# Attention followed by a soft mixture of experts on one core: weight loads spread evenly and cut into short packets, the first three pairs' steps as a written list, idle products on a tile of ones

## The chip, the cores and the metric

The kernel runs on one core of a Trainium2 chip. The metric is the device time of one execution in microseconds, lower is better; the median of the runs counts. TensorE (PE) multiplies, VectorE (DVE), ScalarE (ACT) and GpSimd (POOL) work on its results, and SyncE (SP) and POOL start transfers between the chip's main memory (DRAM) and the core's working memory.

## What is computed

```python
# q, k, v: (8 batches, 12 heads, 448 tokens, 64)
scores = scale * np.matmul(q, k.transpose(0, 1, 3, 2))
m = np.max(scores, axis=-1, keepdims=True)
e = np.exp(scores - m)
attn = e / (np.sum(e, axis=-1, keepdims=True) + np.exp(-m) + 1e-09)
x = np.matmul(attn, v)                       # regrouped to (3584, 768)

logits = x @ phi                             # 32 slots = 8 experts x 4
d = softmax of logits over the 3584 tokens;  c = softmax over the 32 slots
slot_input = d.T @ x                         # (8, 4, 768)
h = np.maximum(slot_input[e] @ w1[e], 0.0)   # w1: (8, 768, 1024)
slot_out[e] = h @ w2[e]                      # w2: (8, 1024, 768)
out = c @ slot_out                           # (3584, 768), float32
```

## The kernel before

**Pairs.** The 96 heads are handled as 48 pairs (`NPAIR`). A pair `n` passes through these steps, each a function that emits instructions at the place where it is called; the order on each engine is the order of the calls.

- `T(n)`, L240: 28 transposes on PE bring q and k into `ps_t`; ACT (L262) or DVE copies them out. Three pairs share one load of q, k and v (a group).
- `A(n, i)`, L273: score products (L284, L293, L303) of one block of 128 queries into `ps_a`, and a maximum over the keys on DVE (L286, L297, L306). Three `ps_a` buffers exist, so PE waits for DVE. `As(c)` takes the next `c` of these steps off the list `runs`.
- `W1(g)`, L309, on POOL, turns the maxima of a group of pairs into a bias; `W2(g)`, L331, transposes it on PE (`ps_m`); `W3(g)` copies it on ACT (`mT`) and forms `exp(-m)`.
- `Bk(n, i)`, L351: score products with keys on the partitions, plus a product that adds the bias (L366 and L369, or L395 and L398), in `ps_b`; ACT takes the exponential (L371, L401). Four buffers, shared with `T`, `W2` and `PX`. In the middle of the kernel an `A` step of a later pair is woven in (`mix`).
- `AV(n, i, qs)`, L420: products with v into the one `ps_av` buffer (L435), for each of four key blocks `i` six products for three blocks of queries and two for the last.
- `N1(n)`, L442: `ps_av` is copied to `ubuf` (L448). `N2(n)`: reciprocal on DVE, multiplications on POOL (L468, L478, L479). `PX(n)`: transposes of the result (L500) and an ACT copy (L506).
- `V(g)` copies a group's v on POOL.

`P(b)` is the part of the mixture that belongs to one batch (six pairs): logits (`ps_l`, L534), running maxima, exponentials, `slot_input` sums.

**Order.** Before the loop: 22 products on a zeroed tile `wm[0]` (L692), then `T(0)`, four `A`, `T(1)`, `W1(0)`, v, `T(2)`, `W2(0)`, `W3(0)`, and loads. Then a loop over slots `s` = 0 to 48 with two halves each; slot `s` does the `Bk` of pair `s`, the second half of `AV` and the `N1`, `N2` of pair `s - 1`, `A` of pairs some three ahead and, from slot 2 on, `T(s + 6)`. Slots 0 to 2 go through the same loop with special cases (`early`, `hs == 1`, `hs < 5`).

**Loads.** All loads that convert from float32 to bfloat16 are issued by POOL and run through one queue of the DMA engines (`gdma`); SP starts those that need no conversion. The 16 expert matrices are halves of six or eight rows per partition; eleven of them (`halves` 0 to 10: all w1 and w2 of experts 0 to 2) have their own place from the start, and are loaded in two parts each: number 0 before the loop, number `half_at[s]` in slots `s + 1`. The last five lie over the attention's buffers, as 40 rows per partition: they are loaded when these come free (`load_rows`, `rows_at`), and some are converted ahead into a DRAM tile (`stage_rows`, L141, its transfer L145, at the slots in `stage_at`) and later fetched from there by SP (`fetch_rows`, L153). w2 is read as `(p j) f`: a partition's rows follow each other in DRAM.

**The end.** After the attention come two groups of four experts: `hidden` (L848), `turn` (transposes of `h`, L860), `slots` (`ps_so`, L867), and the output rows (L904, L906, L910) with 13 stores by SP.

Of the kernel before, what the change touches and what calls it, by code (L numbers as in the profile page):

```python
# [8 lines left out]
F32 = mybir.dt.float32  # L9
# [22 lines left out]
def kernel(  # L32
# [77 lines left out]
    def load_part(i, z0, z1):  # L110
        kind, e = halves[i]
        src = (moe_w1 if kind == "w1" else moe_w2)[e].rearrange("(j p) f -> p j f" if kind == "w1" else "(p j) f -> p j f", p=128)
        gdma(out=w_sb[(kind, e)][:, z0:z1, :], in_=src[:, z0:z1, :])  # L113
# [27 lines left out]
    def stage_rows(r0, r1):  # L141
        i, z = divmod(r0, FK)
        assert r1 <= (i + 1) * FK
        t = dram.tile([128, r1 - r0, DD], BF16, name=f"stage{r0}")
        gdma(out=t, in_=moe_w2[11 + i - E].rearrange("(p j) f -> p j f", p=128)[:, z:z + r1 - r0, :])  # L145
        staged[r0, r1] = t
# [9 lines left out]
    with ExitStack() as at:  # L156
# [532 lines left out]

        ps = psV.tile([128, 512], F32, tag="v", name="ps_idle")  # L690
        for _ in range(22):
            nc.tensor.matmul(ps[:, 0:64], wm[0][:, 0, :], wm[0][:, 0, 0:64], start=True, stop=True)  # L692
        T(0)
        As(2)
        T(1)
        As(2)
        W1(0)
        V(0)
        load(1, "v")
        ones_in(vp[1], nc.gpsimd)  # L700
        As(1)
        T(2)
        W2(0)
        W3(0)
        As(1)
        for nm in "qk":
            load(2, nm)
        for z in range(2):
            load_half(0, z, w_tile(0))

        half_at = {s: i + 1 for i, s in enumerate((1, 4, 7, 10, 13, 19, 22, 28, 31, 34))}


        rows_at = {77: 3, 83: 7, 85: 12, 89: 17, 91: 20, 92: 24, 93: 26, 95: 27}
        rows = 0
        stage_at = {18: (16, 24), 37: (27, 32), 38: (32, 36), 40: (36, 40)}
        wait_loads = []
        waits = [r for z in stage_at.values() for r in range(*z)]  # L720
        for s in range(NPAIR + 1):
            for y in range(2):
                hs = 2 * s + y
                early = int(hs < 4)
                mix = s >= 3 and len(runs) > 1 and runs[0][1] == 1 - y
                if mix:
# [4 lines left out]
                if mix:  # L731
                    pass
                elif s < NPAIR:
                    Bk(s, 2 * y)
                    As(early)
                    side = int(y == 1 and len(runs) > 0 and runs[0][1] == 3)
                    Bk(s, 2 * y + 1, side)
                    As(1 - side)
                else:
                    As(1)  # L740
                if hs == 1:
                    W1(1)
                if hs < 5:
                    T(hs + 3)
                if y == 0:
                    if 0 <= s - 1:
                        for i in (2, 3):
                            AV(s - 1, i, range(3))
                else:
                    if 2 <= s < NPAIR - 6:  # L750
                        T(s + 6)
# [19 lines left out]
                else:  # L771
                    if 0 <= s - 1 and on_pool(s - 1):
                        N2(s - 1)
                As(early)
                if hs == 1:
                    W2(1)
                    W3(1)
                if y == 0 and s and s + 1 in firsts:
# [4 lines left out]
                if y == 0 and s % 3 == 2 and (s + 1) // 3 < NG:  # L783
                    if s == 2:
                        load(2, "v")
                    if s == NPAIR - 4:
                        V(NG - 1)
                    if s - 1 in half_at:
                        load_half(half_at[s - 1], 0, w_tile(half_at[s - 1]))
                if y == 0 and hs in rows_at:  # L790
                    load_rows(rows, rows_at[hs])
                    rows = rows_at[hs]
            def slot_loads(s):
                g = (s + 10) // 3
                if s == 1 or (s and s % 3 == 2):
                    if g < NG:
                        load(g, "q")
                        load(g, "k")
                g = (s + 9) // 3
                if s % 3 == 0 and g - 2 < NG - 1:  # L800
                    V(g - 2)
                    if s and g - 1 < NG:
                        load(g - 1, "v")
                if s - 1 in half_at:
                    load_half(half_at[s - 1], 1)
                if s in stage_at:
                    stage_rows(*stage_at[s])

            if s > 2 and s + 2 in firsts:
# [45 lines left out]
        def turn(g):  # L855
            n = FK // (1 + g)
            for k0 in range(0, FK, n):
                ps = psA.tile([128, n, 128], BF16, tag="a", name="ps_ht")
                for kt in range(k0, k0 + n):
                    nc.tensor.transpose(ps[:, kt - k0, :], h[g].rearrange("p (d k) -> p k d", k=FK)[:, kt, :], ident)  # L860
                (nc.scalar.copy if g and not k0 else nc.vector.tensor_copy)(hT[g][:, k0:k0 + n, :], ps)
# [155 lines left out]
```

## Time and profile before

| | |
|---|---|
| runs | 299.71, 300.39, 301.83 us; median 300.39 |
| profiled execution | 300.82 us, of which span (first to last instruction) 299.0 |
| busy of the span | PE 272.7, DVE 249.7, ACT 250.7, POOL 193.3 |
| maximum on DVE, one alone; six in a row | 0.615; 3.28 |
| 28 transposes, at 9.98 us; at 18.25 us | 0.96; 0.63 |
| exponential on ACT, L371; L401 | 0.575; 0.572 |
| software queue (q0) | 42.29 MB, 35072 packets |
| instruction queue (q8) | 0.66 MB, 40 packets |
| staging of rows 16 to 23 (L145) | 1536 KB, 13.0 us from issue to landing |
| expert weights, 24 transfers | 768 KB each, median 10.1 us to landing |

A timeline row gives the start (us from the span's start), the duration from the first to the last of its instructions, engine, line, operation, what is written and read, the count, and in brackets the engine's idle time before it and what ended that. "issue" stands where the profile names nothing that the engine waited for. A piece of the chain of waits has its start, its length, engine and line. PEld is the loading of PE's stationary operand.

### The profile page before, as it was taken

What the parts mean: (1) busy time and instruction counts of PE and PEld (TensorE: products, weight loads), DVE (VectorE), ACT (ScalarE), POOL (GpSimd) and SP (SyncE); (2) the same over time, 40 slices, a digit from 0 to 9 for tenths busy, and PEclk for the clock granted to TensorE, in tenths of its full rate; (3) what the DMA queues carried; (4) which work ended last, traced back from release to release, by engine and by line L of the source; (5) the groups of instructions that cost most, each with busy time, mean ns of one, the idle gap of its engine ahead of it and who ended that gap; (6) DMA issues with size and microseconds to landing.
All of it is one profiled execution on the core that took longest, in us unless ns stands there. A gap on an engine that the chain in (4) does not pass through costs nothing.

```text
span 299.0 us, 12393 instructions
## 1 busy us (share of the span) xinstructions
PE 272.7 (91%) x5174; PEld 162.8 (54%) x5174; DVE 249.7 (83%) x581; ACT 250.7 (84%) x559; POOL 193.3 (65%) x389
## 2 busy tenths in 40 slices
PE   5989999999999999899999999999999999996810
PEld 4434556565666566557566666666565556652100
DVE  5889799999999999899999999998999675437930
ACT  4567999999899989898999899989999987337820
POOL 8791997879778959886969697978775633000000
PEclk9999999999999999999999999999999999997555
DMA  7999799999999978999998999999999689808997
GB/s 137 142 145 208 115 207 207 209 207 207 193 189 171 197 101 120 193 189 207 210 153 113 151 192 162 194 178 207 181 196 197 120 177 266 329 4 323 380 448 322
DMA packets 40103, 58.67 MB, mean 196 GB/s; under 512 B 2752, under 2 KB 30912, under 8 KB 39744
## 3 DMA queue, kind: packets, MB, share of 16 engines
q0 software_dynamic: 35072, 42.29, 85.8%
q1 hardware_dynamic: 4976, 15.60, 13.3%
q8 instruction: 40, 0.66, 0.8%
q14 instruction: 15, 0.12, 0.1%
HBM read 89.16 MB, written 15.14 MB: 349 GB/s over the span
## 4 chain that ended last, share of the span: by engine, by line
PE 73%; ACT 11%; DVE 5%; issue 3%; POOL 2%; DMA 1%; DVEq 0%; POOLq 0%; ACTq 0%
PE ps_av L435 16%; PE ps_a L284 11%; PE ps_b L366 8%; PE ps_b L369 7%; PE ps_t L255 6%; PE ps_b L395 5%; PE ps_b L398 3%; PE ps_x L500 3%; PE ps_o L910 3%; ACT W L401 2%; ACT W L262 2%; DVE mx L297 2%; ACT W L506 2%; PE ps_s L622 2%; PE ps_h L848 2%
## 5 line engine op out<-in xcount | busy, mean ns | idle before, releaser
L286 DVE TENSOR_REDUCE mx<-ps_a 128x1 f32<-128x448 f32 x250 | 137.4, 613 | 5.2 <-PE ps_a L284 4.4
L371 ACT ACTIVATE W<-ps_b 128x448 bf16<-128x448 f32 x250 | 120.4, 575 | 0.0
L284 PE MATMUL ps_a<-W 64*128 64x448 bf16 x250 | 80.8, 352 | 0.1
L366 PE MATMUL ps_b<-W 64*128 64x448 bf16 x250 | 70.2, 352 | 1.3
L369 PE MATMUL ps_b<-mT,sel 64*128 64x448 bf16 x250 | 66.3, 350 | 0.1
L435 PEld LDWEIGHTS <-W 128*128 128x128 bf16 (+1 forms) x1536 | 50.3, 100 | 27.4 <-issue 23.6
L435 PE MATMUL ps_av<-W 128*128 128x65 bf16 (+1 forms) x1536 | 64.5, 196 | 0.3 <-issue 0.3
L468 POOL TENSOR_TENSOR W<-ubuf,rec 128x384 bf16<-128x384 f32 x44 | 36.3, 826 | 38.6 <-ACT W L506 19.2
L401 ACT ACTIVATE W<-ps_b 128x448 bf16<-128x448 f32 x86 | 45.5, 572 | 4.2 <-PE ps_b L398 4.2
L255 PEld LDWEIGHTS <-W 64*64 64x64 bf16 x1344 | 29.2, 112 | 13.0 <-issue 4.7
L506 ACT CAST W<-ps_x 128x512 bf16<-128x512 f32 x47 | 28.6, 607 | 6.4 <-PE ps_x L500 6.1
L255 PE MATMUL ps_t<-ident,W 64*64 64x64 bf16 x1330 | 30.4, 195 | 2.6 <-ACT W L214 1.3
L306 DVE TENSOR_REDUCE mx<-ps_a 128x1 f32<-128x448 f32 x48 | 29.5, 615 | 1.5 <-PE ps_a L303 1.5
L284 PEld LDWEIGHTS <-W 64*128 64x128 bf16 x250 | 23.3, 94 | 9.8
L369 PEld LDWEIGHTS <-sel 64*128 64x128 bf16 x250 | 19.5, 94 | 14.8 <-issue 6.0
L395 PE MATMUL ps_b<-W 64*64 64x448 bf16 (+1 forms) x134 | 26.9, 374 | 0.3
L113 POOL DMA_DIRECT2D W<-in_moe_w_dram x30 | 20.9, 698 | 7.7 <-PE ps_b L398 7.7
L262 ACT COPY W<-ps_t 128x896 bf16<-128x896 bf16 x21 | 19.6, 933 | 7.2 <-PE ps_t L255 7.2
L448 ACT COPY ubuf<-ps_av 128x455 f32<-128x455 f32 x44 | 25.1, 571 | 0.3
L398 PE MATMUL ps_b<-mT,sel 64*64 64x448 bf16 (+1 forms) x134 | 24.9, 354 | 0.2
L297 DVE TENSOR_REDUCE mx<-ps_a 128x1 f32<-128x448 f32 x38 | 20.9, 616 | 2.1 <-PE ps_a L293 2.1
L479 POOL TENSOR_TENSOR W<-ubuf,rec 128x128 bf16<-128x128 f32 x44 | 17.6, 400 | 3.7
(156 smaller groups left out, 447.2 us busy)
## 6 DMA issues: line engine op xcount, KB each, us to landing
W<-in_moe_w_dram POOLq DMA_DIRECT2D x24, 768.0 KB, 10.1
W<-in_v_dram POOLq DMA_DIRECT2D x32, 192.0 KB, 6.4
out_dram<-W SPq DMA_DIRECT2D x2, 2688.0 KB, 10.0
W<-in_q_dram POOLq DMA_DIRECT2D x15, 336.0 KB, 6.2
W<-in_k_dram POOLq DMA_DIRECT2D x15, 336.0 KB, 7.2
out_dram<-W SPq DMA_DIRECT2D x6, 384.0 KB, 3.0
out_dram<-W SPq DMA_DIRECT2D x3, 768.0 KB, 4.9
W<-stage SPq DMA_DIRECT2D x3, 576.0 KB, 5.6
```

The source lines that it names most:

```text
L255: nc.tensor.transpose(o, src[r, pl, tok * D:(tok + 1) * D], ident[r, r])
L284: nc.tensor.matmul(ps[:, 0:S], t[r, 0, i * 128:(i + 1) * 128], t[r, 1, :], start=True, stop=True)
L286: nc.vector.reduce_max(m[:, c:c + 1], ps[:, 0:S], axis=AX.X)
L366: nc.tensor.matmul(pss[hl][:, 0:S], t[rs[hl], 1, cols], t[rs[hl], 0, :], start=True, stop=False)
L369: nc.tensor.matmul(pss[hl][:, 0:S], sel[rs[hl], 2 * pl + hl:2 * pl + hl + 1].to_broadcast([64, 128]), mT[mg(n)][rs[hl], :], start=False, s ...
L371: nc.scalar.activation(e[:, hl, :], pss[hl][:, 0:S], AF.Exp, scale=scale)
L395: nc.tensor.matmul(outs[hl], t[rs[hl], 1, cols], t[rs[hl], 0, :], start=True, stop=False)
L398: nc.tensor.matmul(outs[hl], sel[rs[hl], 2 * pl + hl:2 * pl + hl + 1].to_broadcast([64, m]), mT[mg(n)][rs[hl], :], start=False, stop=True)
L401: nc.scalar.activation(e, p[:, 0:S], AF.Exp, scale=scale)
L435: nc.tensor.matmul(o, eT[n, i, hl][:, qc], vp[g % 2][:, 2 * pl + hl, i, 0:W65], start=(i == 0 and u == 0 and hl == 0) or (u == 3 and i == ...
L468: eng.tensor_mul(x[:, 0:3, c:c + 128].rearrange("p i (h d) -> p i h d", h=2), u[:, 0:6, 0:D].rearrange("p (i h) d -> p i h d", h=2), rec[: ...
L506: nc.scalar.copy(xT(b, pb), pss[0])
```

## The change

1. `load_part` reads w2 of experts 0 to 3 (halves 8 to 10, and rows 0 to 7 of the 40) as `(j p) f`: partition `p` has rows `p`, `128 + p`, and so on, so each packet is one row. `turn(0)` reads `h[0]` in the order that fits, contiguous columns instead of every eighth.
2. The DRAM tile of `stage_rows` gets 32 unused columns a row, so each of its rows is a packet of its own.
3. `half_at` is every third slot from 4 to 31 instead of ten slots from 1 to 34, and the second part of a half moves from the end of slot `s + 1` to the first half of slot `s + 2`. `stage_at` has the rows 16 to 23 at 34 instead of 18, in two pieces; rows 27 to 31 in two pieces; rows 32 to 39 at 40 in two pieces. First pieces go out in slot `s + 1`, second pieces in slot `s + 2`.
4. The 22 products on `wm[0]` become 48 on the program's constant tile of ones (written at the program's begin), and two of 128 columns follow `T(0)`.
5. The steps before the loop and slots 0 to 2 become one written list, `ramp`; the loop begins with slot 3.

```diff
-        src = (moe_w1 if kind == "w1" else moe_w2)[e].rearrange("(j p) f -> p j f" if kind == "w1" else "(p j) f -> p j f", p=128)
+        src = (moe_w1 if kind == "w1" else moe_w2)[e].rearrange(
+            "(j p) f -> p j f" if kind == "w1" or e < E // 2 else "(p j) f -> p j f", p=128)
...
-        t = dram.tile([128, r1 - r0, DD], BF16, name=f"stage{r0}")
+        t = dram.tile([128, r1 - r0, DD + 32], BF16, name=f"stage{r0}")[:, :, 0:DD]
...
-        ps = psV.tile([128, 512], F32, tag="v", name="ps_idle")
-        for _ in range(22):
-            nc.tensor.matmul(ps[:, 0:64], wm[0][:, 0, :], wm[0][:, 0, 0:64], start=True, stop=True)
-        T(0)
-        As(2)
-        T(1)
-        As(2)
-        W1(0)
-        V(0)
...
+        one = nc.const_aps.tensor(1.0, [128, 512], BF16)
+        ps_idle = psV.tile([128, 512], F32, tag="v", name="ps_idle")
+
+        def idle(n, cols):
+            for _ in range(n):
+                nc.tensor.matmul(ps_idle[:, 0:cols], one[:, 0:128], one[:, 0:cols], start=True, stop=True)
+
+        idle(48, 64)
...
-        half_at = {s: i + 1 for i, s in enumerate((1, 4, 7, 10, 13, 19, 22, 28, 31, 34))}
+        half_at = {s: i + 1 for i, s in enumerate(range(4, 32, 3))}
...
-        stage_at = {18: (16, 24), 37: (27, 32), 38: (32, 36), 40: (36, 40)}
+        stage_at = {34: [(16, 20), (20, 24)], 37: [(27, 29), (29, 32)], 40: [(32, 36), (36, 40)]}
...
+        ramp = ("T0 I A A T1 A A W0 T2 A G0 A X0 J0 A B0.0 A B0.1 A A T3 A B0.2 A A T4 C0.3 V0.0 W1 A V0.1 V0.2 A X1 T5 "
+                "A B1.0 A K0 V0.3 H0 C1.1 N0 B1.2 A T6 C1.3 V1.0 V1.1 A B2.0 M0 K1 A T7 B2.1 A V1.2 V1.3 W2 T8 H1 A "
+                "N1 B2.2 Y2 V2.0 X2 C2.3 Z0 V2.1 M1 K2 ")
...
-        for s in range(NPAIR + 1):
+        for s in range(3, NPAIR + 1):
...
+                if y == 0 and s - 1 in stage_at:
+                    stage_rows(*stage_at[s - 1][0])
+                if y == 0 and s - 2 in half_at:
+                    load_half(half_at[s - 2], 1)
+                if y == 0 and s - 2 in stage_at:
+                    stage_rows(*stage_at[s - 2][1])
...
-                if s - 1 in half_at:
-                    load_half(half_at[s - 1], 1)
-                if s in stage_at:
-                    stage_rows(*stage_at[s])
...
-                    nc.tensor.transpose(ps[:, kt - k0, :], h[g].rearrange("p (d k) -> p k d", k=FK)[:, kt, :], ident)
+                    nc.tensor.transpose(ps[:, kt - k0, :], h[g].rearrange("p (d k) -> p k d" if g else "p (k d) -> p k d", k=FK)[:, kt, :],
+                                    ident)
```

In the list `T`, `A`, `N` (`N1`), `M` (`N2`), `W` (`W1`) are the steps above, `X` is `W2` and `W3`, `B` a `Bk` and `C` a `Bk` with an `A` step inside, `V` an `AV` of three query blocks, `H` the four `AV` of the last query block, `I` the two idle products, `G` the copy of v for group 0 with the next load of v, `J` the loads of q and k of group 2 and of half 0, `K` a slot's loads, `Y` the load of v of group 2, `Z` the first `PX`.

## The prediction

> **What bounds the kernel now.** First the slices of the page: in each row a digit is the busy share of 1/40 of the span (7.5 us).
>
> ```profile
> PE   5989999999999999899999999999999999996810
> DVE  5889799999999999899999999998999675437930
> ACT  4567999999899989898999899989999987337820
> ```
>
> Three stretches: a start of four slices in which nobody is full, a long middle in which PE is full but for one slice (the 17th, near 125 us), and an end that the change hardly touches. Next the chain of waits, where the six logit products of each batch (`ps_l`, L534) come once every six pairs and so serve as a clock of the middle:
>
> ```profile
> 59.71 0.59 PE ps_l L534 x24
> ...
> 88.63 0.59 PE ps_l L534 x24
> ...
> 117.59 0.59 PE ps_l L534 x24
> ...
> 147.79 0.59 PE ps_l L534 x24
> ...
> 176.81 0.59 PE ps_l L534 x24
> ```
>
> The steps are 28.92, 28.96, 30.20 and 29.02 us: a steady PE pace of 4.83 us a pair, and one batch that lost 30.20 - 28.95 = 1.25 us. The timeline of that batch has the loss:
>
> ```profile
> 125.69 0.35 PE L255 MATMUL ps_t<-ident,W 64*64 64x64 bf16 x11 [0.87 <-issue]
> ...
> 127.06 3.28 DVE L286 TENSOR_REDUCE mx<-ps_a 128x1 f32<-128x448 f32 x6 [1.09 <-PE ps_a L284]
> ```
>
> PE stopped for 0.87 us in the middle of 28 transposes of data that had landed by 102. "issue" says that no engine and no load held it. In the packet records the instruction queue (q8, 16 KB a packet) asks every 6 to 7 us, but here it goes from 113.7 to 123.5; between lies the staging load of L145 (issued at 116.7, 1536 KB, 13.0 us to landing), whose packets are 32 KB, the largest of the run. I read it as PE waiting for its next instructions behind those packets.
>
> Last, VectorE in the start:
>
> ```profile
> 11.97 0.62 DVE L306 TENSOR_REDUCE mx<-ps_a 128x1 f32<-128x448 f32 x1 [0.92 <-PE ps_a L303]
> ...
> 20.98 3.28 DVE L297 TENSOR_REDUCE mx<-ps_a 128x1 f32<-128x448 f32 x6 [0.67 <-PE ps_a L293]
> 24.70 0.62 DVE L306 TENSOR_REDUCE mx<-ps_a 128x1 f32<-128x448 f32 x1 [0.43 <-PE ps_a L303]
> ...
> 31.92 1.16 DVE L297 TENSOR_REDUCE mx<-ps_a 128x1 f32<-128x448 f32 x2 [0.48 <-PE ps_a L293]
> ...
> 34.51 0.62 DVE L286 TENSOR_REDUCE mx<-ps_a 128x1 f32<-128x448 f32 x1 [0.60 <-PE ps_b L366]
> 35.63 1.16 DVE L286 TENSOR_REDUCE mx<-ps_a 128x1 f32<-128x448 f32 x2 [0.49 <-PE ps_a L284]
> ```
>
> From its first maximum (5.73) to 35.63 DVE does 46 maxima at a pitch of 0.547 us (six in 3.28) and two reciprocal steps, 25.7 us, and idles 4.2 us: the six gaps shown and 0.36, 0.18, 2 x 0.04. PE and ACT idle more (ACT 8.0 us from 8.20 to 29.36), then ACT has no gap at all from 29.36 past 36. So the start is DVE's queue, starved where PE has other work ahead of a score product, with ACT late at its end.
>
> **The list of first steps.** The work of pairs 0 to 2 is the same; from pair 3's first score product on, PE's order is that of before. So the start is worth what that point moves, and the PE-paced middle passes it on. Gap by gap: 0.36 is the landing of pair 1's k and stays. 0.92 came because 28 transposes (0.96) and the mask products stood between A(1,0) and A(1,3); now they stand behind A(0,1) and A(0,2), whose four maxima are 2.2 us of cover: gone. 0.18 and 0.67 came from W2(1), which waits for GpSimd's W1(1), itself behind four load issues until 19.69; the loads stay there, but A(3,1) and A(3,2) now stand ahead of W2(1): some 0.15 is left. 0.43 came from transposes and 20 value products ahead of A(4,3); these are now cut into sixes and twelves between A's: gone. The last three (1.57) come where ACT frees `ps_b` buffers late. ACT's work is no smaller: I worked the engines' queues through in program order with the rows' own pitches (maximum 0.547, exponential 0.425, transposed copy 0.80, pair of score products 0.19, 28 transposes 0.44, or 0.89 before 14 us, GpSimd's rows as they are, loads landing as they did). That puts the four copies of `ubuf` (L448; rows 24.47, 31.86, 37.18, 41.88) at 24.1, 31.3, 36.7, 41.4 for before, and at 23.8, 29.7, 34.5, 39.2 for the new order, with one DVE gap of 1.25 near 31, where A(6,3) waits behind pair 2's last scores for a buffer. Left are 0.36 + 0.15 + 1.25 = 1.75 of 4.2, a gain of 2.45; the copies give 2.2. I take **-2.3**. Bounds: -3.85 if only the 0.36 stays; 0 if ACT and the landings give all back, for T(6) and T(9) now come 0.5 and 0.4 us behind their landings (before: T(9) at 38.0).
>
> **Idle products.** 22 took 1.36 us, 0.055 each once running; 48 take 0.2 + 47 x 0.055 = 2.8 us. Their operand is written by GpSimd at 0.31 instead of DVE at 0.86, so they run from about 0.8 to 3.6, and T(0) waits for its cast until 3.82: hidden by 0.2 us; without that cover +0.2. The two of 128 columns (0.11 each) sit in PE's 0.39 us of waiting for the first copies. What they may bring is the clock. The page shows full clock from the start, but 28 transposes take 0.96 at 9.98 and 0.63 at 18.25, a lone score product 0.53 and then 0.35: the array is slow until about 14.5. By the same working, full speed from 7 instead of 14 moves the end of the start by 0.2, from 4 by 0.6, for DVE and the landing of q, k of group 1 (14.0) hold it anyway. I count 0.1 in the -2.3; bounds +0.2 and -0.6.
> [...]
>
> **Loads.** The staging of rows 16 to 23 moves from slot 18 to slots 35 and 36, in two halves; every staged row is now a 1536-byte packet; the w2 halves of experts 0 to 3 go from 6144 to 1536 bytes. The 32 KB packets are gone, so the 1.25 goes: **-1.2**. A smaller stop of 0.35 at 213.7 stands in the same kind of load (7680-byte packets): **-0.2**. Bounds: 0 (the stop has another cause) and -1.6. What replaces them: halves now go out every three slots from slot 4 to 31. The software queue runs one transfer after another: a half lands 3.7 us behind the one before it, q or k 1.7, v 1.0 twice; three slots need 2 x 3.7 + 2 x 1.7 + 2 x 1.0 = 12.8 of 14.5 us. Packet size hardly shows: 512 bytes at 195 GB/s, 896 at 200, 2048 and 6144 at 207 to 210. At 195 three slots need 13.3: hidden. If that cover went, the price would be what 14.5 is exceeded by, ten times; for 1 us a half must take 3.7 + 0.9. GpSimd issues 512 pieces for 128 (0.63 us; 384 pieces take 0.78, so some 0.85): six halves, expert 3's rows and the staging, +0.2 each on an engine 65% busy whose loads land far ahead: its next work behind them is N2, whose result PX needs a slot later. 0. The worst landing (k, 13.4 us, at 137.4) was still some 6 us ahead of its transposes. The rows (32, 36) and (36, 40) are staged 3 and 1 slots later; the queue stood empty near 238 to 240, which takes it. SP has one fetch more at 0.32.
> [...]
>
> **The end.** `h[0]` is transposed from contiguous columns instead of every eighth: eight take 0.71 in either group now, 0; bounds +-0.1.
>
> **Sum.** -2.3 - 1.2 - 0.2 = -3.7. The profiled execution took 300.82 (span 299.0, 1.8 around it), which gives 297.1; it lay 0.4 over the median 300.39, which gives **296.7**.
>
> **Rivals.**
> 1. The start gives it back: ACT, gapless from 29.36 on, or T(6) and T(9) at their landings, starve DVE as before. For it: the 1.25 gap that was worked out and the thin 0.4 to 0.5 us; against: the same working meets the rows of before within 0.5. Only the loads pay: -1.4, 299.0. Chance 0.13.
> 2. The stop stays or moves: the instruction queue still waits behind staging, now at slots 35 to 42. For: it has one packet every 6 to 7 us whatever the loads; against: the w2 halves with 6144 bytes show no stop. -2.4, 298.0. Chance 0.10.
> 3. More: DVE keeps only the 0.36 (-3.85), and the loads -1.4: 295.1. Against it is ACT's gapless stretch. Chance 0.12.
> 4. Slower: the last fetches. From 251 to 262 SP fetches 13 staged rows (2.6 MB) at some 400 GB/s, 6.4 us of transfer, and the second group's products use the last at about 266, 4 us after it landed. Rows now come as 1536-byte packets out of padded rows instead of 4.6 to 7.7 KB. At a third of the rate the 6.4 us become 19.2 and overrun by 8.8; with the -3.7 that is +5.1, 305.5. It costs below 250 GB/s and outweighs the gain below 180. Against: output stores are 1536-byte packets already, and 384 KB land 0.5 us after 192 KB do (3.0, 2.5), 390 GB/s. Chance 0.05.
>
> **Numbers.** The forecast has 0.60, reaching from 295.6 to 298.2 by the bounds of its terms. About 1% (3 us, 297.4) is what a measurement can tell; five sixths of the forecast lie under it, so faster 0.50 + 0.12 = 0.62; slower 0.05; the rest, 0.33, within. The range leaves out the slower case and some of the ends: 294.9 to 299.2.
>
> **What would show it.** Right: L448's first four copies near 23.9, 30.1, 35.0, 39.7; DVE idle under 2.3 us up to pair 3; the `ps_l` steps all within 28.8 to 29.1; no "issue" wait of PE over 0.3 in the middle. Wrong: a step still over 29.5; ACT or a landing releasing several DVE gaps before 30 us; `ps_so` products waiting for a load.

## The result, and the profile after

| | before | after |
|---|---|---|
| median (runs) | 300.45 us (20) | 298.94 us (20) |
| ratio, 95% interval | | 0.9946, 0.9924 to 0.9968 |
| profiled execution, span | 300.82, 299.0 | 300.67, 298.9 |

By the ratio, which compares the means of the runs without the few that lie over 1.5% above the fastest of their kernel, the change saves 1.6 us (1.0 to 2.3), where 3.7 were forecast. The profiled execution lies 1.7 us over the median of its kernel, so its lines show more waiting than most executions have; runs further below tell which of it belongs to the program.

The slices of the page, one digit for 7.5 us:

```profile
PE   7989899999999999999889999999999999996810
...
DVE  6999789999999989999889999999999675537930
ACT  4569989999899979998989899989999987337810
...
PEclk9599999999999999999999999999999999998555
```

PE's hole in the 17th slice is gone, and two new ones stand in the 20th and 21st (near 142 to 157 us). In the start the third slice has its 8 still, and the fifth (30 to 37 us) has an 8 where it was full. The clock row has full speed in the first slice and half of it in the second; the trace's record of the clock begins at 4.72 in this execution, and the row counts the time before it as full.

The chain of waits of the changed kernel (start, length, engine, line):

```profile
4.37 6.58 DMA W<-in_v_dram
...
17.55 7.30 DMA W<-in_k_dram
...
30.88 7.09 DMA W<-in_k_dram
...
59.15 0.59 PE ps_l L535 x24
...
88.07 0.59 PE ps_l L535 x24
...
117.68 0.59 PE ps_l L535 x24
...
147.15 0.59 PE ps_l L535 x24
...
177.50 0.59 PE ps_l L535 x24
```

Two things answer to the prediction. The chain now runs through the load of k of group 2 and that of group 3, transfers that the forecast had left as they were. And the first batch's logits come 0.56 us earlier (59.71 to 59.15), but the steps after that are 28.92, 29.61, 29.47 and 30.35, not 28.8 to 29.1: at 177.50 the kernel is 0.69 later than before.

The first four copies of `ubuf` by the timeline (forecast: 23.9, 30.1, 35.0, 39.7; before: 24.47, 31.86, 37.18, 41.88):

```profile
24.48 0.55 ACT L449 COPY ubuf<-ps_av 128x455 f32<-128x455 f32 x1
...
30.68 0.61 ACT L449 COPY ubuf<-ps_av 128x455 f32<-128x455 f32 x1
...
35.89 0.59 ACT L449 COPY ubuf<-ps_av 128x455 f32<-128x455 f32 x1
...
41.44 0.60 ACT L449 COPY ubuf<-ps_av 128x455 f32<-128x455 f32 x1
```

At the first copy nothing is won, at the second and third 1.2 to 1.3 us; at the fourth 0.44 are left. The gaps of VectorE there, in the same view:

```profile
10.00 1.16 DVE L298 TENSOR_REDUCE mx<-ps_a 128x1 f32<-128x448 f32 x2 [0.38 <-PE ps_a L294]
...
21.73 1.16 DVE L298 TENSOR_REDUCE mx<-ps_a 128x1 f32<-128x448 f32 x2 [0.31 <-PE ps_a L294]
...
30.45 1.16 DVE L298 TENSOR_REDUCE mx<-ps_a 128x1 f32<-128x448 f32 x2 [0.48 <-PE ps_a L294]
...
32.98 0.62 DVE L307 TENSOR_REDUCE mx<-ps_a 128x1 f32<-128x448 f32 x1 [1.37 <-PE ps_a L304]
```

Five of the six gaps that the prediction showed are gone or smaller. The sixth stands unchanged: 0.48 us ahead of the 43rd maximum, at 31.92 before and at 30.45 here. In all VectorE idles 2.9 us up to pair 3, where under 2.3 were forecast. A gap of 1.37 stands where the forecast expected one of 1.25, but its cause is another, as the first two rows of PE's own waits show:

```profile
31.34 0.34 PE L436 MATMUL ps_av<-W 128*128 128x65 bf16 x6 [0.62 <-ACT ubuf L449]
...
32.24 0.34 PE L336 MATMUL ps_m<-ident,W 128*128 128x128 bf16 x3 [0.56 <-POOL W L314]
...
38.01 0.41 PE L256 MATMUL ps_t<-ident,W 64*64 64x64 bf16 x14 [0.93 <-DMA W<-in_k_dram]
...
105.10 0.34 PE L336 MATMUL ps_m<-ident,W 128*128 128x128 bf16 x3 [0.58 <-POOL W L314]
...
142.72 0.35 PE L285 MATMUL ps_a<-W 64*128 64x448 bf16 x1 [0.44 <-DVE mx L287]
...
149.74 0.57 PE L256 MATMUL ps_t<-ident,W 64*64 64x64 bf16 x24 [0.52 <-issue]
...
156.21 0.22 PE L436 MATMUL ps_av<-W 128*128 128x65 bf16 x2 [0.58 <-issue]
```

These are a wait of `AV` for ACT's copy of `ps_av`, waits for GpSimd's bias (`W2`, twice), one for a landing (`T(9)`), and three stops in the middle, two of them with no releaser. None of the seven stands at its place in the profile of before. The first two lie ahead of the score product that ends the gap of 1.37 (L304, near 32.55). The prediction had that product wait behind pair 2's last scores for a buffer; here 0.56 of its delay is a wait for GpSimd that the forecast didn't have. That the size agrees is luck: without that wait the gap is 0.64 (e5_behind, below).

### The profile page after: what moved, and what is told of

Same layout as the page of the kernel before. It is cut to its first block, busy times and chain, and to the rows that moved or that the text cites. A ratio compares the mean times of both kernels' runs of the same rounds, so it can differ in the third digit from the quotient of the medians.

```text
span 298.9 us, 12454 instructions
## 1 busy us (share of the span) xinstructions
PE 271.9 (91%) x5202; PEld 164.0 (55%) x5202; DVE 249.5 (83%) x581; ACT 250.0 (84%) x559; POOL 196.1 (66%) x391
## 4 chain that ended last, share of the span: by engine, by line
PE 71%; ACT 9%; DMA 7%; POOL 5%; issue 3%; DVE 1%; DVEq 0%; POOLq 0%; ACTq 0%
PE ps_av L436 16%; PE ps_a L285 11%; PE ps_b L367 8%; PE ps_b L370 7%; PE ps_b L396 5%; DMA W<-in_k_dram 5%; PE ps_t L256 5%; PE ps_x L501 3%; PE ps_b L399 3%; PE ps_o L932 2%; DMA W<-in_v_dram 2%; ACT W L402 2%; PE ps_s L623 2%; PE ps_h L869 2%; ACT W L507 2%
## 5 line engine op out<-in xcount | busy, mean ns | idle before, releaser
L287 DVE TENSOR_REDUCE mx<-ps_a 128x1 f32<-128x448 f32 x250 | 137.2, 613 | 5.1 <-PE ps_a L285 4.3
L114 POOL DMA_DIRECT2D W<-in_moe_w_dram x30 | 22.6, 755 | 7.9 <-PE ps_b L399 7.7
L298 DVE TENSOR_REDUCE mx<-ps_a 128x1 f32<-128x448 f32 x38 | 21.2, 616 | 1.9 <-PE ps_a L294 1.8
```

The source lines that it names most:

```text
L287: nc.vector.reduce_max(m[:, c:c + 1], ps[:, 0:S], axis=AX.X)
```

## The experiments

Three theories stood after this. **A:** the list runs PE up against GpSimd's queue and the landings of groups 2 and 3, which caps the start. **B:** the stops in the middle are accidents of an execution that no load's shape removes, so the 1.4 us for the loads were never to be had. **C:** the clock, which rises early and falls back, takes the gain. The table has all runs; what they are follows below. "Eighth copy" is the start of the eighth copy of `ubuf` in that run's timeline, by which the start is over; "middle" is the time from the first batch's `ps_l` row to the seventh's; "stops" is the sum of PE's stops at a code boundary between 60 and 240 us (below).

| run | median | ratio to before, interval | eighth copy | middle | stops |
|---|---|---|---|---|---|
| before | 300.45 | | 60.64 | 174.6 | 1.22 |
| after | 298.94 | 0.9946 (0.9924 to 0.9968) | 60.08 | 175.2 | 1.54 |
| e8_again (after) | 298.67 | 0.9930 (0.9906 to 0.9954) | 60.03 | 174.0 | 0.60 |
| e1_loads | 300.25 | 0.9984 (0.9958 to 1.0011) | 60.55 | 173.4 | 0 |
| e2_list | 298.64 | 0.9930 (0.9898 to 0.9963) | 59.05 | 174.0 | 0.27 |
| e3_idle22 | 298.72 | 0.9947 (0.9915 to 0.9978) | 58.88 | 174.4 | 0.82 |
| e4_early | 298.17 | 0.9898 (0.9853 to 0.9943) | 58.14 | 174.8 | 1.33 |
| e13_before_early | 300.33 | 0.9961 (0.9930 to 0.9991) | 60.45 | 173.1 | 0 |
| e5_behind | 296.91 | 0.9880 (0.9853 to 0.9907) | 58.15 | 173.2 | 0.28 |
| e14_best (e5_behind) | 296.92 | 0.9858 (0.9822 to 0.9895) | 58.38 | 173.3 | 0.31 |
| e12_oldloads | 297.55 | 0.9880 (0.9840 to 0.9919) | 58.38 | 174.3 | 1.15 |
| e10_longpk | 297.62 | 0.9879 (0.9836 to 0.9922) | 59.88 | 173.9 | 0.76 |
| e9_idle57 | 297.29 | 0.9887 (0.9843 to 0.9931) | 57.90 | 173.8 | 0.97 |
| e11_noidle | 297.45 | 0.9882 (0.9843 to 0.9921) | 58.19 | 173.0 | 0 |
| e6_long | 299.94 | 0.9981 (0.9949 to 1.0013) | 59.97 | 174.9 | 1.46 |
| e7_none | 297.97 | 0.9898 (0.9878 to 0.9917) | 58.41 | 172.8 | 0 |

The medians were taken on several chips, on which before had 300.37 to 301.57; between sets the ratios count.

### The halves of the change: e1_loads, e2_list

e1_loads is the kernel before with parts 1 to 3 of the change and its old start:

```diff
-        src = (moe_w1 if kind == "w1" else moe_w2)[e].rearrange("(j p) f -> p j f" if kind == "w1" else "(p j) f -> p j f", p=128)
+        src = (moe_w1 if kind == "w1" else moe_w2)[e].rearrange(
+            "(j p) f -> p j f" if kind == "w1" or e < E // 2 else "(p j) f -> p j f", p=128)
...
-        t = dram.tile([128, r1 - r0, DD], BF16, name=f"stage{r0}")
+        t = dram.tile([128, r1 - r0, DD + 32], BF16, name=f"stage{r0}")[:, :, 0:DD]
...
-        half_at = {s: i + 1 for i, s in enumerate((1, 4, 7, 10, 13, 19, 22, 28, 31, 34))}
+        half_at = {s: i + 1 for i, s in enumerate(range(4, 32, 3))}
...
-        stage_at = {18: (16, 24), 37: (27, 32), 38: (32, 36), 40: (36, 40)}
+        stage_at = {34: [(16, 20), (20, 24)], 37: [(27, 29), (29, 32)], 40: [(32, 36), (36, 40)]}
```

e2_list is the changed kernel with those lines as before: parts 4 and 5 alone.

> The loads alone (w2 of experts 0 to 3 as single rows, padded staging tile, even half loads, staging later and in pieces, h[0] order), on the kernel before with its old start. As the prediction has it (-1.2 and -0.2): 1.4 us less than before, about 299.0, every step of ps_l (L534 of before) within 28.8 to 29.1 and no issue stop of PE over 0.3 us in the middle. If the stops stay or move (rival 2): 0 to -0.5 us, with stops of 0.4 to 0.6 us elsewhere.

> The list of first steps and the idle products alone, with the loads of before (also the first half at slot 1, so the list's load lines issue part of half 1). As the prediction has it (-2.3): 298.1. If the start gives it back at the landings of groups 2 and 3, as the trace of the changed kernel suggests (net -0.6 at the last copies of ubuf): about 299.8, with a wait of PE for the load of k of about 0.9 us in T(9). The stop of 1.25 us at 125 should be there in full.

The loads alone give 0.5 us, with an interval from 1.3 faster to 0.3 slower that the forecast's 1.4 lies just outside; the list alone gives 2.1 (1.1 to 3.1), all that the whole change gives. And the stop of 1.25 us that was to stand "in full" in e2_list isn't there: its staging transfer at 115.56 has the same 32 KB packets, and PE runs through it. The same staging passes without a stop in e6_long, e12_oldloads and e13_before_early. So the stop near 125 in the profile of before was no part of the program.

What the loads do add is a wait. In e1_loads, GpSimd by the timeline:

```profile
94.97 0.83 POOL L176 DMA_DIRECT2D W<-in_q_dram  x1 [0.74 <-PE ps_b L370]
95.81 0.78 POOL L176 DMA_DIRECT2D W<-in_k_dram  x1
96.60 0.53 POOL L591 TENSOR_TENSOR z<-lb,lb 128x160 f32<-128x160 f32 x1
97.08 0.78 POOL L114 DMA_DIRECT2D W<-in_moe_w_dram  x1
...
105.22 0.31 POOL L314 TENSOR_SCALAR W<-mx 128x36 bf16<-128x36 f32 x1
105.50 0.28 POOL L314 TENSOR_SCALAR ngm<-mx 128x21 bf16<-128x21 f32 x1
```

and PE, in the same view:

```profile
105.59 0.34 PE L336 MATMUL ps_m<-ident,W 128*128 128x128 bf16 x3 [0.58 <-POOL W L314]
```

From 94.97 to 105.77 GpSimd has no gap. Its step of L314, for which `W2` waits, ends at 105.53, and PE has stood for 0.58. In the kernel before, GpSimd has no gap there either:

```profile
94.27 0.82 POOL L175 DMA_DIRECT2D W<-in_q_dram  x1
95.09 0.78 POOL L175 DMA_DIRECT2D W<-in_k_dram  x1
95.86 0.78 POOL L113 DMA_DIRECT2D W<-in_moe_w_dram  x1
...
104.52 0.31 POOL L313 TENSOR_SCALAR W<-mx 128x36 bf16<-128x36 f32 x1
```

The step (L313) ended at 104.83 and `W2` began at 105.02 without a wait: the margin was 0.2 at most. An issue of a half (L113, L114) stands in the stretch in both kernels, so it isn't what the new order added. What it added is the 0.74 ahead of the load of q, which begins 0.70 later than before. This is a pause of GpSimd itself; it stands at this very issue in all five profiles with this order of loads (after, e1, e3, e4, e8), and not in the five with the order of before (before, e2, e6, e12, e13), which pause for 0.62 at a load of v near 87 instead, ahead of 0.8 to 1.5 us of idle time that takes it up. What GpSimd does there, no run tells (the name after the arrow is only the last event before it).

### A second profile: e8_again

> The changed kernel itself once more, for a second profile and a median beside the others of this set. If its first profile's stops in the middle (0.44, 0.52 and 0.58) and the wait of 0.93 in T(9) are parts of the program: they stand again at the same products. If they are accidents of one execution: the W2 wait of 0.58 near 104 stays, the others are gone or elsewhere. Time 298.9.

The three stops of the middle are gone (another, of 0.60, begins at 90.84), so they don't belong to each execution. The `W2` waits stand again (0.56 from 31.19, 0.53 from 105.24), and so does `T(9)`, with 1.29 for 0.93.

### Where the stops come from, and whether packets matter: e10_longpk, e6_long, e7_none

The trace settles the stops' nature. Number PE's records (matmuls, weight loads and eight of its sequencer) from 0 at the start of the span: the stops of before stand at numbers 4545 and 8129, those of after at 5313, 5569 and 5825, each 193 past a multiple of 256. The instruction queue has one packet of 16 KB for every 256 of these records (40 packets for 10,356). By this each stop reads as PE at the end of the code that it has, with the next 16 KB late: in before PE passes the boundary at number 4289 at 118.17, the next packet comes from 123.46 to 124.44, and PE, idle from 124.82, goes on at 125.69. The first stop of after, which the timeline puts down to VectorE (L287), is of the same kind, as its 5313 shows.

How late is a packet, and does it depend on what it waits behind? From the moment when PE passes one boundary to the start of the next packet, over the 15 profiles that have all loads, by the packet size that made up most bytes of the load queue meanwhile:

| load packets, bytes | code packets | mean delay, us | stops | time lost, us |
|---|---|---|---|---|
| 512 (v) | 84 | 1.90 | 0 | 0 |
| 896 (q, k) | 86 | 2.99 | 3 | 1.57 |
| 1536 (w2 and staging, new) | 70 | 2.84 | 2 | 1.00 |
| 2048 (w1) | 121 | 3.06 | 11 | 5.43 |
| 4608 to 7680 (old) | 50 | 3.07 | 5 | 1.86 |
| 32768 (old staging) | 7 | 3.83 | 1 | 0.87 |

(Where a code packet waits behind two sizes, the row depends on the rule: if the loads still under way count too, the last row has nine packets and two stops, 1.28 us.) A code packet waits some 3 us behind loads of nearly any size (v, in the smallest transfers, apart; behind 32 KB it is longest, by 0.8 us, on few packets). No stop came below 3.15 us of delay, and three of the four packets later than 4.4 made one. Half of the stops fall behind w1, whose packets the change leaves alone; one of seven packets behind 32 KB made one. The stops aren't spread evenly: the boundaries at numbers 3009, 3265 and 5313 hold eleven of the 22, the last of them in five profiles (0.15 to 1.33 us). So the place is in part the program's; whether PE stops there, and for how long, changes from one execution to the next. For the packets that the change replaced it is 6 stops in 57 (the last two rows), for those in their place 2 in 70, too few to tell a small gain from none. If shorter packets let code through sooner, the trace shows little of it: 2.84 us behind 1536 bytes, 3.07 behind 4608 to 7680.

Two runs test it by time. e10_longpk is the best kernel (e5_behind, below) with the row order and the staging tile of before; its staging goes out in pieces, so its longest packets are 6144 bytes, and none has 32 KB: it tests 1536 bytes against 6144. e6_long is e2_list with a second staging transfer of 32 KB packets:

```diff
-        src = (moe_w1 if kind == "w1" else moe_w2)[e].rearrange(
-            "(j p) f -> p j f" if kind == "w1" or e < E // 2 else "(p j) f -> p j f", p=128)
+        src = (moe_w1 if kind == "w1" else moe_w2)[e].rearrange("(j p) f -> p j f" if kind == "w1" else "(p j) f -> p j f", p=128)
...
-        t = dram.tile([128, r1 - r0, DD + 32], BF16, name=f"stage{r0}")[:, :, 0:DD]
+        t = dram.tile([128, r1 - r0, DD], BF16, name=f"stage{r0}")
```

```diff
             if s in stage_at:
                 stage_rows(*stage_at[s])
+            if s == 27:
+                gdma(out=dram.tile([128, 8, DD], BF16, name="again"), in_=moe_w2[5].rearrange("(p j) f -> p j f", p=128))
```

> e5_behind with the packets of before: w2 of all experts read as (p j) f, the staging tile without the unused columns, h[0] in the order of before. The times of the loads are those of e5_behind. If long packets stop PE (the prediction): stops of 0.3 to 1.2 us near the six w2 halves and the staging, 0.5 to 1.5 us slower than e5_behind. If the packet size does nothing: within 0.4 us of e5_behind, 296.9, and the code packets' mean lag is 2.6 to 3.1 us again.

> The kernel with the list and the old loads (e2_list) and the suspected cost doubled: a second staging transfer of 1536 KB in 32 KB packets, at slot 27, into a tile that nobody reads. If 32 KB packets stop PE as the prediction has it: one more stop of 0.9 to 1.25 us near 165, so 1 us slower than e2_list, 299.6. If the stops depend on when a code packet happens to be late, not on the packets' size: within 0.4 us of e2_list, and code packets start 2.5 to 4.2 us after PE has passed the boundary before, behind packets of any size.

With packets of up to 6144 bytes the best kernel has the same ratio, 0.9879 for 0.9880, each with some 1 us either way, so a loss of 0.5 us isn't excluded. (Its profile is a late one, 1.6 us over its median: PE waited 1.27 us for k of group 1 at 13.7, and the clock was back at half from 14.4 to 21.2. The 59.88 of the table comes from these two, in shares that one profile doesn't tell.) e6_long is slower than e2_list by 1.5 us by the ratios, with an uncertainty nearly as large, which by itself would fit the prediction; but its profile shows no stop of 0.9 us or more at the second staging. The first code packet behind that staging's 32 KB packets came 4.09 us after its boundary, and PE ran on. PE's waits in its timeline:

```profile
86.08 0.34 PE L255 MATMUL ps_t<-ident,W 64*64 64x64 bf16 x10 [1.05 <-issue]
...
163.65 0.34 PE L335 MATMUL ps_m<-ident,W 128*128 128x128 bf16 x3 [0.33 <-POOL W L313]
...
174.38 0.25 PE L435 MATMUL ps_av<-W 128*128 128x65 bf16 x3 [0.41 <-issue]
```

The largest stop, 1.05, falls at 85, where the queue carries q, k, v and w1; the one of 0.41 has its code packet waiting from 168.2 to 172.2, some half of it behind the last 32 KB packets of the second staging and half behind packets of 6144 bytes, so the staging may have a share in it. The rest is a wait of 1.00 in `T(9)` and two `W2` waits (0.33 above, 0.36 at 193) for a GpSimd with one issue more. How these share in the median, one profile can't tell.

e7_none leaves ten halves out, which bounds all that their order or shape could gain:

```diff
-            w_view(i, t)
+            w_view(i, w_tile(0))
+        if i:
+            return
```

> The kernel with the earlier loads of groups 2 and 3 (e4_early), without the loads of the expert matrices' halves 1 to 10: their products read half 0's place, so ten loads of 1536 KB and their GpSimd issues are left out of the middle. It bounds what any order, size or packet of these loads could gain. If PE's stops come from code packets that wait behind the loads: no issue stop of over 0.2 us between 60 and 200, code packets start earlier (mean lag under 2 us, against 2.6 to 3.1), the W2 wait goes, and the time falls by 1.0 to 1.9 us against e4_early. If the loads cost nothing in the middle: no change.

No stop, a mean delay of 1.31 us for 2.61 in e4_early, and a middle of 172.8 us, the shortest of all. Against the 174.6 of before's profile the loads could gain 1.8 us, if they were free; e11_noidle and e13_before_early, with all loads, have 173.0 and 173.1. The time as a whole doesn't fall by the 1.0 to 1.9 us that were expected: the ratio is that of e4_early, 0.9898. In the profile the end, from the last batch's logits on, is 1.1 us longer than in e4_early; why stays open. The stops cost 0.82 us a profile on average with the loads of before (before, e2, e6, e12, e13) and 0.65 with the new ones (nine profiles), each profile between 0 and 1.54. This fits theory B: with neither shape of the loads are the profiles free of stops, and leaving the loads out freed them. Six transfers of staging in 32 KB packets, in the five profiles with the loads of before, have at most 1.28 us of stops behind them, 0.2 each, where the prediction counted 1.25.

### What caps the start: e4_early, e13_before_early

The loads of q and k of group 2 are issued right behind `T(2)`, ahead of the copy of v; those of group 3 right behind group 0's next v, ahead of the first `N2`:

```diff
-        ramp = ("T0 I A A T1 A A W0 T2 A G0 A X0 J0 A B0.0 A B0.1 A A T3 A B0.2 A A T4 C0.3 V0.0 W1 A V0.1 V0.2 A X1 T5 "
-                "A B1.0 A K0 V0.3 H0 C1.1 N0 B1.2 A T6 C1.3 V1.0 V1.1 A B2.0 M0 K1 A T7 B2.1 A V1.2 V1.3 W2 T8 H1 A "
+        ramp = ("T0 I A A T1 A A W0 T2 A Q G0 A X0 J0 A B0.0 A B0.1 A A T3 A B0.2 A A T4 C0.3 V0.0 W1 A V0.1 V0.2 A X1 T5 "
+                "A B1.0 A K0 K1 V0.3 H0 C1.1 N0 B1.2 A T6 C1.3 V1.0 V1.1 A B2.0 M0 A T7 B2.1 A V1.2 V1.3 W2 T8 H1 A "
...
+            elif op == "Q":
+                for nm in "qk":
+                    load(2, nm)
             elif op == "J":
-                for nm in "qk":
-                    load(2, nm)
                 for z in range(2):
```

> The changed kernel with the loads of q and k of groups 2 and 3 issued earlier on GpSimd: group 2 ahead of v's copy of group 0, group 3 ahead of the last value products of pair 0. If the landings cap the start (theory A): the waits of T(6) and T(9) for the loads go (0.93 us in T(9) in the changed kernel's profile) and the time falls by 0.6 to 1.0 us to about 298.1. If the start is capped by ACT or DVE anyway: no change (within 0.2 us), the fourth copy of ubuf still near 41.4 us. If earlier transfers push other landings (v of group 1) or GpSimd's copies back: up to 0.5 us slower.

The eighth copy comes at 58.14, 1.9 us earlier than in the changed kernel. The ratio is 0.9898 beside 0.9946 and 0.9930, so the time falls by some 1.0 to 1.4 us, with an uncertainty about as large. The causes are seen in GpSimd's queue, by the timeline of the changed kernel:

```profile
30.04 0.84 POOL L176 DMA_DIRECT2D W<-in_q_dram  x1 [0.43 <-PE ps_t L256]
30.88 0.78 POOL L176 DMA_DIRECT2D W<-in_k_dram  x1
31.68 0.22 POOL L318 TENSOR_TENSOR W<-mx,nhalfm 128x12 bf16<-128x12 f32 x1
31.86 0.32 POOL L314 TENSOR_SCALAR W<-mx 128x36 bf16<-128x36 f32 x1
```

and of e5_behind, which has the same start as e4_early:

```profile
22.43 0.83 POOL L176 DMA_DIRECT2D W<-in_q_dram  x1
23.25 0.79 POOL L176 DMA_DIRECT2D W<-in_k_dram  x1
...
29.04 0.21 POOL L318 TENSOR_TENSOR W<-mx,nhalfm 128x12 bf16<-128x12 f32 x1
29.53 0.30 POOL L314 TENSOR_SCALAR W<-mx 128x36 bf16<-128x36 f32 x1 [0.28 <-DVE mx L298]
```

In the list, `W1(2)` stands behind two load issues and ends 2.3 us later than with the early loads, and `W2(2)` waits for it; this wait, 0.55 to 0.57, is in all five profiles with the list and the late loads (after, e2, e3, e6, e8). And k of group 3, issued at 30.4 to 30.9, takes 5.5 us to land in one of them, 6.3 in another and 7.1 to 7.5 in three: `T(9)`, which PE reaches near 37, waits 0, 0.17, 0.93, 1.00 and 1.29. With the early loads, k of group 3 lands at 32.4 to 34.7 and neither wait is left. The first four copies of e5_behind are then those of the forecast (23.9, 30.1, 35.0, 39.7) within 0.4:

```profile
24.23 0.54 ACT L449 COPY ubuf<-ps_av 128x455 f32<-128x455 f32 x1
...
30.16 0.61 ACT L449 COPY ubuf<-ps_av 128x455 f32<-128x455 f32 x1
...
34.67 0.70 ACT L449 COPY ubuf<-ps_av 128x455 f32<-128x455 f32 x1
...
39.39 0.78 ACT L449 COPY ubuf<-ps_av 128x455 f32<-128x455 f32 x1
```

VectorE idles 1.7 us up to pair 3 there, as the forecast had it (1.75), but in other gaps: 0.40, the unchanged 0.48, and, in place of the 1.25,

```profile
31.72 0.62 DVE L307 TENSOR_REDUCE mx<-ps_a 128x1 f32<-128x448 f32 x1 [0.64 <-PE ps_a L304]
```

Whether the early loads make this without the list was asked with the kernel before:

```diff
+        for nm in "qk":
+            load(2, nm)
         V(0)
...
+                if hs == 2:
+                    load(3, "q")
+                    load(3, "k")
```

> The kernel before with nothing but the loads of q and k of groups 2 and 3 issued earlier on GpSimd (no list, loads and idle products of before; PE's order is the same). If the list and the landings work together, so that an earlier landing pays only where the list has run PE up to it: no gain, 300.4, ratio 0.997 to 1.003, the eighth copy of ubuf near 60.6 as before. If the earlier loads alone made the gain of e4_early and e5_behind: 1.5 us or more faster, under 299, and that copy under 59.5.

By the copies they don't: the eighth moves by 0.1 to 0.2 (60.45; 60.64 and 60.55 with the old start), though k of group 3 lands 3.5 us earlier. The ratio, 0.9961, is a little better than the 0.997 expected; the profile has its gain in a middle without a stop (173.1), and one profile doesn't settle more. By the copies of the start the list and the landings work together: 1.6 to 1.8 us at best for the list alone, 0.2 for the landings alone, 2.3 to 2.5 for both. The times can't show it, for the list's 2.1 us and these 1.2 (0.3 to 2.1) add up to 3.3, beside 3.6 for both (e12_oldloads, below).

### The wait of W2, and a faster kernel: e5_behind, e14_best, e12_oldloads

e5_behind is e4_early with both parts of a half issued together, behind `W1`:

```diff
                     if s - 1 in half_at:
                         load_half(half_at[s - 1], 0, w_tile(half_at[s - 1]))
+                        load_half(half_at[s - 1], 1)
...
-                if y == 0 and s - 2 in half_at:
-                    load_half(half_at[s - 2], 1)
```

> The kernel with the earlier loads of groups 2 and 3 (e4_early), in which both parts of a half are issued together behind W1, in slots 5, 8 and so on, instead of the second part one slot later. Every profile with the new loads has one wait of PE of 0.58 us in W2 (L336, near 104) for GpSimd, which runs gapless there from the loads of q and k to W1, with one of the half's issues (0.78 us) between. If that issue is the cause: the wait goes, the 26.5 us between two batches' logits near 102 becomes 25.85, and the time is 0.6 us under e4_early, about 297.5. If GpSimd's work there is late for another reason: the wait stays, no change. If q and k now land late, behind two parts of a half: waits of T for loads, slower by 0.5 or more.

The `W2` wait is gone in both its profiles (e14_best is the second), and the step between the two batches' logits (L535) on either side of it, 29.62 us in e4_early, is 29.41 and 28.96. It has the lowest median of the study: 3.6 us under before (2.8 to 4.4), 1.8 under the changed kernel in the same set (e8_again). Two things went from GpSimd's stretch at once, the half's issue and the pause of 0.74 (one of 0.55 now stands near 165.6, where nobody waits). This run doesn't part them, but the profiles with the loads of before do: all five have such an issue in this stretch, none has the pause, and in none does `W2` wait. So it was the pause that made the wait; taking the issue out as well leaves GpSimd more room.

> e5_behind once more, for a second profile beside e13. If its gain rests on the program and not on one profile's luck: 296.9 within 0.6, ratio 0.985 to 0.991, no wait of PE for a load of k before 40 us, no W2 wait near 104, the eighth copy of ubuf within 0.3 of 58.15.

A second set bears it out, 296.92 and 0.9858; the eighth copy is 0.23 later, all else as expected.

> e2_list (the list, the loads of before) with the earlier loads of q and k of groups 2 and 3: what e4_early is with the new loads. If the landings cap the start (theory A), the waits of T(6) and T(9) go here too, and the last copy of ubuf in the start (the eighth) stands near 58.1 as in e4_early and e5_behind (e2_list 59.05). The time is then what e5_behind is without the new loads: by the middle stretches of the profiles (173.2 in e5_behind, 174.0 in e2_list, 174.6 before) 0.5 to 1.4 us more than e5_behind, 297.4 to 298.3. If the new loads bring nothing once the W2 wait is gone: 296.9.

The same start with the loads of before has the same ratio as e5_behind, 0.9880. (Its median of 297.55 lies where the first branch of the expectation put it, but before was slower in that set too, and the ratio is that of the second.) So parts 1 to 3 of the change bring nothing that can be measured, even without the wait that they caused; the intervals are some 1 us either way.

### The idle products and the clock: e3_idle22, e9_idle57, e11_noidle

e3_idle22 is the changed kernel with the idle products of before, e9_idle57 is e5_behind with nine more, e11_noidle is e5_behind with none:

```diff
-        idle(48, 64)
+        for _ in range(22):
+            nc.tensor.matmul(ps_idle[:, 0:64], wm[0][:, 0, :], wm[0][:, 0, 0:64], start=True, stop=True)
...
-        idle(48, 64)
+        idle(57, 64)
...
-        idle(48, 64)
```

In the first and the last the list begins "T0 A A" in place of "T0 I A A".

> The changed kernel with the 22 products on the zeroed tile of before and without the two of 128 columns. If the early idle products bring what the prediction counted (0.1 us, bounds -0.6 to +0.2): 0 to 0.3 us slower than the changed kernel, with full clock only from about 14 us. [...] If they cost (T(0) later): 0.2 us faster.

> e5_behind with 57 idle products instead of 48, which fills PE's wait of 0.48 us for the cast before T(0). In six profiles with the 48, the full clock came near 4 us in two, and fell back 3.4 us later; in all it came for good between 12.3 and 15.2. If the wait before T(0) breaks the busy time that the clock needs: full clock from about 4 us on, 0.2 to 0.6 us less than e5_behind. If the clock goes by something else: no change, and it comes for good after 12 us again.

> e5_behind without any idle products. If the idle products are worth what the prediction counted (0.1 us more than the 22 of before, whose worth is not known): 0 to 0.5 us slower, the clock for good after 12 us all the same. If they bring nothing: within 0.2 us.

22, 48, 57 or none: the ratios are 0.9947 (22) beside 0.9946 and 0.9930 (48), and 0.9887 (57) and 0.9882 (none) beside 0.9880 (48). The trace's record of the granted clock says why theory C has little to take. In most profiles with the 48 the full clock comes once, between 12.3 and 13.2 us; without them, or with the 22, between 14.0 and 15.0, and the 2 us between are worth nothing that the times show. In the profile of after it comes at 4.72, falls back at 8.13 and returns at 14.96 (so the page's row has 9, 5, 9); e4_early has the same from 3.5 to 6.9, e9_idle57 from 5.8 to 9.2, where the expectation had it for good. Each run's mean clock tells how often this happens: of the changed kernel's 20 runs ten have 0.945 to 0.952, as the profile with the fall has (0.948), and ten 0.957 to 0.962. Their medians are 299.3 and 298.9 us. Over all runs with 48 or 57 products those with such a low mean take 0.5 us longer on average (37 runs against 48, uncertain by about as much). So theory C can hold a few tenths, not the 2 us that are missing.

## Why the prediction was right and wrong

**The sign, and the list as the source:** right. The list of first steps makes the gain as far as it can be measured (2.1 us in e2_list, 0.5 in e1_loads with an interval that includes 0), and five of the six gaps of VectorE are gone or smaller.

**"The 32 KB packets are gone, so the 1.25 goes" (-1.2, and -0.2 at 213.7):** this is the step that failed. What the stop was, PE waiting for code behind loads, was right; that it was tied to these packets rested on one stop in one profile. Twenty-two stops in 15 profiles fall behind packets of nearly every size, three of them (0.39 and 0.53 us in e12_oldloads, 0.17 in e10_longpk) behind halves of 6144 bytes, which the prediction had as free of stops. The term of -1.4 measured -0.5 (-1.3 to +0.3) with the old start, the new `W2` wait included, and between 0.7 us faster and 0.5 slower with the new one, where the intervals are some 1 us either way. It is rival 2 ("the stop stays or moves"), but with stops that come and go between executions in place of a fixed new spot.

**"GpSimd ... its next work behind them is N2 ... 0":** wrong. Behind N2 comes `W1`, for which PE waits in `W2`, and near 104 GpSimd had a margin of 0.2 us at most. The pause of 0.74 that came with the new order used it up: +0.6 us in every profile of the changed order. The longer issues that the prediction priced are not what did it. The share of 65% busy hid how thin the margin was.

**-2.3 for the list, "loads landing as they did":** the size was right where the loads don't hold PE: the four copies came within 0.4 once the loads went out earlier, and the eighth copy then moved by 2.2 to 2.7 (e10_longpk with its late start apart). In part that is luck, for the gaps that make up the 1.75 left are others than the prediction named: a 0.48 that was to go stays, and the 1.25 is 0.64, behind ACT's copy of `ps_av`. With the list and the late loads the eighth copy moved by 0.6 to 0.7 (the three profiles with a long `T(9)` wait) or 1.6 to 1.8 (the other two). The prediction had put `T(9)` only 0.4 us behind its landing, and named it as rival 1. It took the landing of one profile, where the time from issue to landing varies by 2 us, and it looked at `W1(1)` in GpSimd's queue, not at `W1(2)`. Rival 1's other half, ACT, has no part in this difference: PE's wait of 0.62 us for ACT's copy of `ps_av` near 31 is there with the late loads and with the early ones.

**Idle products, 0.1:** not contradicted, and not shown either: none of the variants could be told apart, and 0.1 us is far below what the sets resolve. Full speed from 7 or from 4 us, from which the gain and its bound of -0.6 were worked out, was the author's assumption, and no run shows it: for good it came at 12.3 us or later, and where it came at 3.5 to 5.8 it fell back.

**The end, and rival 4 (fetches at a third of the rate):** the last fetch lands 1.4 us later (263.47 for 262.03) and no product waits. From the last logits to the first `ps_so` it is 12.6 us before and 12.5 after.

**The sum:** 3.7 became 1.6 (2.1 in e8_again): next to nothing in place of the 1.4 for the loads, and 1.6 to 2.1 in place of the 2.3 for the start, whose size the times don't contradict. Two slips in the working change nothing: at 195 GB/s the loads of three slots take 13.6 us, not 13.3, still under 14.5; and 0.1 of rival 2's -2.4 is worked out nowhere.

## What to carry to other kernels

A stop in one profile is not yet a part of the program: look whether it stands again in another execution before a change is priced by it, and look in the trace for its kind (here the record's number, modulo 256). A forecast whose size comes out can still have the wrong parts in it: compare gap by gap. When an order of work is tightened, walk the issuing engine's queue too, with every step that another engine waits for, and give each landing its spread instead of one value. An engine with a third of its time free can still have stretches of 10 us without a gap (GpSimd in e1_loads, 66% busy, from 94.97 to 105.77).

## What the runs showed of the hardware

PE's code came in packets of 16 KB on a DMA queue of its own (q8). Without the ten halves (e7_none) a packet started on average 1.31 us after PE had passed the boundary before; with them it was 2.61 in e4_early and, between 60 and 240 us, 2.81 in before and 2.69 in after. A stop ended 1.2 to 1.7 us after the packet's own end (124.44 to 125.69 in before). The same load of 336 KB, issued at 30.4 to 30.9, landed 5.5 to 7.5 us later in five executions of four kernels that differ little up to there. GpSimd paused at some load issues: 0.74 us near 95 in the five profiles with the new order of loads named above, 0.62 near 87 in the five with the order of before; the cause is open. And the clock's early release lasted 3.41 us in three profiles (after, e4_early, e9_idle57) and 10.2 in a fourth (e10_longpk), and didn't come at all in seven others with the 48 products; what brings it, no run here shows.
